# A chunked scan that feeds an FFN: another hand-written list for the lead-in

## The chip, the cores and the metric

The kernel runs on one core of a Trainium2 chip. The metric is the device time of one execution in microseconds; a time of a kernel is the median of its runs. TensorE (PE; its weight loads are shown apart as PEld), VectorE (DVE), ScalarE (ACT), GpSimd (POOL) and SyncE (SP) each work through an instruction list of their own, in order, and wait for one another by semaphores. SyncE here only issues DMAs.

## The reference

The input is a scan with 4 batches of 8 heads over 768 positions, head width 32 and state width 16, and an FFN behind it on 3072 tokens (256 wide, 2048 hidden). Cut to what matters:

```python
log_a = np.log(np.clip(a, 1e-06, 1.0))
for c in range(nc):                       # chunks of positions, in order
    cum = np.cumsum(la, axis=-1)
    L = np.exp(cum[..., :, None] - cum[..., None, :]) * causal
    M = np.einsum('bhin,bhjn->bhij', Cc, Bc) * L
    y[:, :, sl] = M @ xc + (Cc @ state) * np.exp(cum)[..., None]
    state = decay_full * state + sum_j(Bx_j * decay_from_j)
x = y.transpose(0, 2, 1, 3).reshape(B * S, H * D)
h = x @ w_in
return np.maximum(0.01 * h, h) @ w_out
```

## The kernel before

The kernel takes its own chunks of 48 positions, so 16 of them, c = 0 to 15. The steps of a chunk, with the names that the lists use:

- `decN` (L302; `maskN`, L284, and `directN`, L294, for chunks 0 to 2): matmuls that put the sums of log a between two positions into a PSUM bank. `expN` (L321, L326) takes their exponential on ScalarE into `lt`. For chunks from 3 on the operands `dl` and `dr` come back from DRAM (`saveN`, `rowsN`) and are filled on chip (`fl`, `fr`, `cols`).
- `scN` (L347, 16 matmuls of fp32, 32 in the trace): C times B. `weighN` (L361, VectorE) multiplies them into `lt`. `sdN` (L332, GpSimd) puts the state's part into `lt`.
- `pN` (L378, 32 matmuls, 64 in the trace): the products with `xs`, which hold x and, in some rows, the state. `turnN` (L409, VectorE) transposes the new state and `hI` (L422, one of eight copies a chunk, on ScalarE, VectorE or GpSimd) hands it on to the next chunk's `xs`: p2 needs chunk 1's copies.
- `highsN` (L431) and `lowsN` (L439) split a chunk's outputs into a high and a low half, since the FFN is done as three products (high by high, low by high, high by low). The weights of one of the 16 hidden slices arrive packed (`wS`), are decoded by `abs` (L458, ScalarE), `shift` (L471), `sign` (L476) and `low` (L485, VectorE), and are split by `wh` (L496, ScalarE) and `wl` (L499, VectorE or GpSimd).
- `hpS` (L537): slice S of the hidden layer for 512 tokens, six matmuls; `gh`, `act`, `gl` the activation; `opS` (L564) the second product.

Some matmuls do nothing but keep TensorE busy: `du@X:n` is n dummies of 128x512 (`keep_warm`, L139) written into the bank that X will use.

What is done ahead of the main loop is the lead-in. Its order is not planned by a program: `AT_ONCE` (L59) names the DMAs that SyncE issues first, and `LEAD_IN` (L60) is a list of some 300 tokens that a loop (L738 to L753) works through. Each token emits its step, and an engine's list is the order in which the tokens for it were emitted. A letter behind a colon picks the engine (`h6:A`, `wl1:P`). Behind the lead-in (from hp6 on) the main loop sets the order by itself, and the change does not touch it.

PSUM banks are handed out in turn from pools of two: `banks()` (tiles `sc`) and, until the first `hp`, `ps_d` (tiles `pd`). A step that takes a bank waits until the readers of what was last in it are done. `pin`, `pxs` and `wr` hold three chunks of c, three of x and three weight slices.

The fetches on SyncE's queue: `la` 128 KB, each c 448 KB, each w 512 KB, x of chunk 0 256 KB, of later chunks 2 x 96 KB.

The loop that runs the list, for a plain token and for a dummy:

```python
        name, _, host = name.partition("@")
        if host:
            kind = host.rstrip("0123456789")
            keep_warm(space_of(kind, int(host[len(kind):] or 0))[:, 0], int(eng))
            continue
```

Of the kernel before, what the change touches and what calls it, by code (L numbers as in the profile page):

```python
# [55 lines left out]

PD = {0: "d", 1: "d", 2: "d"}
OS = {0: "c", 1: "d", 2: "d"}
AT_ONCE = ["la", "c0", "w0", "x0", "c1"]  # L59
LEAD_IN = """  # L60
less clampn du@mask1:1 lnn clampf reach0:V reach1:V reach3:V top1:P mask0 mask1 after
lnf sums top0:P reach5:V direct0 fl1 sc0 cast0 rest reach2:V revn direct1 reach4:V cast1
exp0 erevn abs0 sd0 du@sc1:2 exp1 part2 fr3:A weigh0 shift0 p0 sel mask2 w1 save0 sc1 x1
fl0 direct2 sign0 c2 turn0 x2 sd1 low0 rows3 h5:P h6:A h3:V h4:P h0:A h2:P h1:A cols
h7:A abs1 weigh1 rev rows4 highs0 shift1 fr4:A sign1 p1 turn1 sd2 sc2 c3 exp2 erevf
du@p2:3 h9:A wh0 lows0 c4 h14:P weigh2 highs1 du@dec3:1 h15:P h13:P dec3 h12:A h8:P dec4
h11:V exp3 h10:V p2 low1 lows1 w2 du@sc3:1 turn2 exp4 highs2 sc3 h22:A rows5 wh1 h21:A
wl0:V h23:A h18:A h20:P lows2 sc4 h17:P x3 abs2 hp0 gh0 sd3 h19:P weigh3 weigh4 wl1:P
hp1 h16:P sd4 act0 shift2 w3 c5 gh1 abs3 dec5 sign2 exp5 gl0 low2 wh2 shift3 act1 sign3
p3 x4 w4 op0 turn3 h29:A low3 h30:P c6 h25:A rows6 highs3 wl2:V sc5 h26:A hp2 h28:A  # L70
h31:P wh3 w5 gl1 op1 h27:A sd5 wl3:P h24:A abs4 gh2 lows3 weigh5 shift4 w6 sign4 act2 p4
save1 turn4 dec6 h35:P h34:P highs4 h33:P h32:P x5 h36:A low4 hp3 abs5 gl2 x6 op2 lows4
wh4 h37:A abs6 w7 rows8 shift5 h38:P wl4:V h39:A c7 gh3 sign5 exp6 shift6 low5 act3 wh5
hp4 gh4 act4 wl5:P rows7 c8 w8 p5 sign6 gl3 turn5 abs7 low6 gl4 sc6 x7 h41:P w9 op3 sd6
highs5 h43:P weigh6 h45:A h42:A h44:P h47:P wh6 wl6:P hp5 h46:P op4 gh5 h40:P act5 lows5
gl5
"""


# [1 line left out]
def scan_ffn(ctx: ExitStack, tc: tile.TileContext, a_l, c_l, x_l, w_l, out_l):  # L81
# [67 lines left out]
    la = pe.tile([128, NC * NM], F32, name="la")  # L149
    for name in AT_ONCE:  # L150
        if name == "la":
# [927 lines left out]
```

## Time and profile before

| | us |
|---|---|
| median of 3 runs (lowest, highest) | 303.19 (302.35, 303.59) |
| profiled execution | 305.16 |
| its span | 302.9 |
| TensorE busy in the span | 296.8 (98%) |
| weight loads of TensorE | 233.0 (77%) |
| VectorE busy | 214.7 (71%) |
| ScalarE busy | 181.8 (60%) |
| GpSimd busy | 66.0 (22%) |

A profile is of one execution. Its span runs from the first instruction to the last; 2.26 us of the execution's own time lie around the span. A busy share is a mean over stages that are limited by different things, so a change in one stage is read from that stage: the timeline of an engine gives, in order, when a group of like instructions starts, how long it takes from its first start to its last end, and in brackets how long the engine idled before it and who ended the wait. Groups overlap a little, because matmuls are pipelined; the distance between two starts is the better price of a group.

### The profile page before, as it was taken

How to read it: one execution, taken by the hardware profiler on the slowest of the kernel's cores; microseconds unless marked ns; L12 is line 12 of the kernel's file. 1: busy time of each engine (PE TensorE's matmuls, PEld its weight loads, DVE VectorE, ACT ScalarE, POOL GpSimd, SP SyncE). 2: the span in 40 equal slices, each digit the busy share in tenths (PEclk: the TensorE clock that was granted, in tenths of full speed). 3: DMA queues.
4: the chain of work that ended last, by engine and by line, in shares of the span. 5: the costliest groups of instructions: out<-in, count | busy, mean ns of one | idle time of the engine just before them, and what ended most of it. 6: DMA issues, size and time to landing. Idle time of an engine off the chain costs nothing.

```text
span 302.9 us, 6809 instructions
## 1 busy us (share of the span) xinstructions
PE 296.8 (98%) x2724; PEld 233.0 (77%) x2724; DVE 214.7 (71%) x379; ACT 181.8 (60%) x348; POOL 66.0 (22%) x141
## 2 busy tenths in 40 slices
PE   8989999999999999999999999999999999999995
PEld 4567777777777778888888888888888888888883
DVE  6589988877676778866877886677566565656562
ACT  4679988576665565835455656673665364536452
POOL 4535565776676430000000000000000000000000
PEclk9999999999999999999999999999999999999999
DMA  7878781965524001000100000000030000000004
GB/s 242 265 214 299 228 263 55 291 193 183 181 89 120 3 2 69 0 2 0 69 2 1 0 0 2 1 0 0 2 139 0 0 2 0 0 1 2 0 0 139
DMA packets 12476, 23.18 MB, mean 77 GB/s; under 512 B 4606, under 2 KB 5502, under 8 KB 12446
## 3 DMA queue, kind: packets, MB, share of 16 engines
q1 hardware_dynamic: 12446, 22.76, 23.5%
q8 instruction: 21, 0.34, 0.4%
q14 instruction: 9, 0.07, 0.1%
HBM read 19.31 MB, written 3.44 MB: 75 GB/s over the span
## 4 chain that ended last, share of the span: by engine, by line
PE 92%; ACT 4%; DVE 2%; issue 1%; DVEq 0%
PE sc L813 18%; PE op L843 14%; PE sc L843 14%; PE op L564 14%; PE hp L537 12%; PE hp L813 7%; PE sc L347 3%; PE sc L378 3%; PE sc L302 1%; ACT xs L422 1%; PE pd L294 1%; PE sc L139 1%; ACT mag L458 1%; PE pd L284 1%; PE pd L378 1%
## 5 line engine op out<-in xcount | busy, mean ns | idle before, releaser
L422 POOL COPY xs<-stage 16x128 f32<-16x128 f32 x96 | 34.5, 360 | 32.4 <-DVE stage L409 24.1
L547 ACT ACTIVATE gh<-hp 128x512 fp32r<-128x512 f32 x32 | 19.1, 597 | 26.8 <-PE hp L537 26.7
L854 ACT ACTIVATE gh<-u 128x512 fp32r<-128x512 f32 x32 | 20.0, 625 | 17.7 <-DVE u L895 17.7
L858 DVE TENSOR_TENSOR gl<-u,gh 128x512 fp32r<-128x512 f32 x32 | 22.0, 687 | 7.9 <-ACT u L855 7.9
L564 PE MATMUL op<-gh,wh 128*128 128x512 f32 x64 | 27.5, 430 | 0.0
L854 ACT ACTIVATE gh<-kept 128x512 fp32r<-128x512 f32 x16 | 10.1, 633 | 28.1 <-DVE kept L903 28.1
L894 DVE TENSOR_TENSOR u<-sc,kept 128x512 f32<-128x512 f32 x16 | 11.1, 691 | 22.2 <-PE sc L813 22.2
L854 ACT ACTIVATE gh<-hp 128x512 fp32r<-128x512 f32 x16 | 9.6, 598 | 26.8 <-PE hp L813 26.8
L564 PE MATMUL op<-gl,wh 128*128 128x512 f32 x64 | 25.1, 392 | 0.0
L564 PE MATMUL op<-gh,wl 128*128 128x512 f32 x64 | 25.0, 391 | 0.0
L843 PE MATMUL op<-gl,wh 128*128 128x512 f32 x64 | 24.9, 389 | 0.0
L843 PE MATMUL sc<-gl,wh 128*128 128x512 f32 x64 | 24.9, 389 | 0.0
L843 PE MATMUL sc<-gh,wl 128*128 128x512 f32 x64 | 24.9, 389 | 0.0
L843 PE MATMUL op<-gh,wh 128*128 128x512 f32 x64 | 24.9, 389 | 0.0
L843 PE MATMUL op<-gh,wl 128*128 128x512 f32 x64 | 24.9, 389 | 0.0
L843 PE MATMUL sc<-gh,wh 128*128 128x512 f32 x64 | 24.9, 389 | 0.0
L903 DVE TENSOR_TENSOR kept<-sc,kept 128x512 f32<-128x512 f32 x16 | 11.1, 692 | 19.4 <-PE sc L813 19.3
L553 DVE TENSOR_TENSOR gl<-hp,gh 128x512 fp32r<-128x512 f32 x32 | 21.7, 677 | 4.3 <-ACT hp L550 4.3
L361 DVE TENSOR_TENSOR lt<-sc,lt 128x384 f32<-128x384 f32 x32 | 16.2, 551 | 12.0 <-ACT gh L547 8.2
L855 ACT ACTIVATE u<-u 128x512 f32<-128x512 f32 x32 | 20.2, 632 | 1.0
L537 PE MATMUL hp<-xh,wh 128*128 128x512 f32 x64 | 20.4, 400 | 0.1
L537 PE MATMUL hp<-xh,wl 128*128 128x512 f32 x64 | 19.9, 392 | 0.0
(142 smaller groups left out, 730.7 us busy)
## 6 DMA issues: line engine op xcount, KB each, us to landing
raw<-w_l SPq DMA_DIRECT2D x16, 512.0 KB
bcn<-c_l SPq DMA_DIRECT2D x16, 448.0 KB
xs<-x_l SPq DMA_DIRECT2D x30, 96.0 KB
out_l<-ob SPq DMA_DIRECT2D x10, 256.0 KB
out_l<-ob SPq DMA_DIRECT2D x4, 128.0 KB
xs<-x_l SPq DMA_DIRECT2D x1, 256.0 KB
dl<-left_d SPq DMA_DIRECT2D x13, 9.0 KB
dr<-right_d SPq DMA_DIRECT2D x13, 9.0 KB
```

Source lines behind the costliest of these rows:

```text
L361: nc.vector.tensor_tensor(out=to, in0=at, in1=to, op=ALU.mult)
L378: nc.tensor.matmul(to[(2 * g + p) * D:(2 * g + p + 1) * D, e, b, cols], lhsT=xs[h * R:(h + 1) * R, 2 * p + e, b], rhs=lt[h * R:(h + 1) * R ...
L422: copy_on(eng)(xss[c + 1][h * R:h * R + N, 2 * p:2 * p + 2, bs], stages[c][rows, :, bs])
L537: nc.tensor.matmul(hp, lhsT=w_half[h][:, f, k * 128:(k + 1) * 128], rhs=x[t][:, k, cols], start=(n == 0), stop=(n == 5),)
L547: nc.scalar.activation(ghs[s], hps[s], AF.Prelu, alpha=0.01)
L553: nc.vector.tensor_tensor(out=gls[s], in0=hps.pop(s), in1=ghs[s], op=ALU.subtract)
L564: nc.tensor.matmul(op, lhsT=w_half[h][:, f, DM + m * 128:DM + (m + 1) * 128], rhs=x, start=(start and i == 0), stop=(last and i == 2),)
L813: nc.tensor.matmul(bank, lhsT=w[h], rhs=x[g], start=start and i == 0, stop=i == 2, skip_group_check=True,)
L843: nc.tensor.matmul(outs[t][m], lhsT=w_half[h][:, f, DM + m * 128:DM + (m + 1) * 128], rhs=x, start=start and i == 0, stop=last and i == 2,)
L854: nc.scalar.activation(gh, h, AF.Prelu, alpha=0.01)
L855: nc.scalar.activation(in_place, h, AF.Prelu, alpha=0.01)
L858: nc.vector.tensor_tensor(out=gl, in0=g, in1=gh, op=ALU.subtract)
```

## The change

Only the two lists differ; every step is done as before, on the same tiles. On SyncE the weight slices w0 and w1 go to the front and chunk 1's c goes behind x0. On GpSimd the zero fill of `top0` comes first, ahead of the selects for `less`; the second fill stays ahead of those for `after`. On ScalarE one fill of `dr` (`fl1`) comes ahead of the logarithms. On TensorE, two dummies come ahead of the first scores, where there were two ahead of chunk 0's products; the mask of chunk 2 comes ahead of chunk 0's products, with a dummy; `revn` comes ahead of `sc0`; chunk 4's decays (`dec4`) come behind chunk 2's products and chunk 3's scores; chunk 4's scores come between `hp0` and `hp1`; chunk 5's decays come behind chunk 3's products. There are seven dummies behind the first four, formerly eight. Of the lead-in's seven `wl`, six now go to GpSimd and wl5 to VectorE; before, wl0, wl2 and wl4 were VectorE's and the others GpSimd's.

```diff
--- before.py
+++ after.py
@@ -56,24 +56,24 @@
 
 PD = {0: "d", 1: "d", 2: "d"}
 OS = {0: "c", 1: "d", 2: "d"}
-AT_ONCE = ["la", "c0", "w0", "x0", "c1"]
+AT_ONCE = ["la", "w0", "c0", "w1", "x0"]
 LEAD_IN = """
-less clampn du@mask1:1 lnn clampf reach0:V reach1:V reach3:V top1:P mask0 mask1 after
-lnf sums top0:P reach5:V direct0 fl1 sc0 cast0 rest reach2:V revn direct1 reach4:V cast1
-exp0 erevn abs0 sd0 du@sc1:2 exp1 part2 fr3:A weigh0 shift0 p0 sel mask2 w1 save0 sc1 x1
-fl0 direct2 sign0 c2 turn0 x2 sd1 low0 rows3 h5:P h6:A h3:V h4:P h0:A h2:P h1:A cols
-h7:A abs1 weigh1 rev rows4 highs0 shift1 fr4:A sign1 p1 turn1 sd2 sc2 c3 exp2 erevf
-du@p2:3 h9:A wh0 lows0 c4 h14:P weigh2 highs1 du@dec3:1 h15:P h13:P dec3 h12:A h8:P dec4
-h11:V exp3 h10:V p2 low1 lows1 w2 du@sc3:1 turn2 exp4 highs2 sc3 h22:A rows5 wh1 h21:A
-wl0:V h23:A h18:A h20:P lows2 sc4 h17:P x3 abs2 hp0 gh0 sd3 h19:P weigh3 weigh4 wl1:P
-hp1 h16:P sd4 act0 shift2 w3 c5 gh1 abs3 dec5 sign2 exp5 gl0 low2 wh2 shift3 act1 sign3
-p3 x4 w4 op0 turn3 h29:A low3 h30:P c6 h25:A rows6 highs3 wl2:V sc5 h26:A hp2 h28:A
-h31:P wh3 w5 gl1 op1 h27:A sd5 wl3:P h24:A abs4 gh2 lows3 weigh5 shift4 w6 sign4 act2 p4
-save1 turn4 dec6 h35:P h34:P highs4 h33:P h32:P x5 h36:A low4 hp3 abs5 gl2 x6 op2 lows4
-wh4 h37:A abs6 w7 rows8 shift5 h38:P wl4:V h39:A c7 gh3 sign5 exp6 shift6 low5 act3 wh5
-hp4 gh4 act4 wl5:P rows7 c8 w8 p5 sign6 gl3 turn5 abs7 low6 gl4 sc6 x7 h41:P w9 op3 sd6
-highs5 h43:P weigh6 h45:A h42:A h44:P h47:P wh6 wl6:P hp5 h46:P op4 gh5 h40:P act5 lows5
-gl5
+top0:P less clampn fl1 mask0 clampf lnn lnf du@mask1:1 fl0 mask1 reach1:V sums cast0
+reach0:V top1:P du@sc0:2 reach4:V reach3:V c1 rest abs0 reach2:V after shift0 cast1
+direct0 part2 revn fr4:A reach5:V exp0 sc0 direct1 sign0 erevn weigh0 du@mask2:1 fr3:A
+mask2 sel low0 exp1 x1 sd0 p0 turn0 sd1 abs1 save0 h1:P h6:P shift1 h5:A h0:P sc1 h4:V
+h3:A weigh1 direct2 h7:A rev c2 h2:A highs0 x2 erevf sign1 p1 turn1 exp2 lows0 sc2 w2
+cols h11:A du@p2:2 h10:A h13:A sd2 h12:P rows3 h15:P h9:P dec3 h8:P weigh2 c3 h14:A wh0
+p2 exp3 low1 rows4 c4 du@dec4:1 turn2 x3 highs1 highs2 rows5 wl0:P lows1 sc3 abs2 dec4
+h19:P lows2 w3 shift2 wh1 exp4 w4 hp0 sign2 save1 h22:A c5 sc4 h23:A rows6 gh0 h16:A
+act0 sd3 wl1:P weigh3 h21:V h17:A h20:P low2 h18:P x4 wh2 weigh4 abs3 gl0 hp1 p3 turn3
+sd4 gh1 wl2:P dec5 w5 abs4 h26:A x5 highs3 shift3 hp2 sign3 op0 h25:P lows3 h24:V h29:A
+act1 h30:A sc5 gh2 exp5 h27:P gl1 low3 shift4 sign4 h31:P w6 act2 wh3 h28:P p4 rows7 c6
+turn4 h32:A op1 gl2 c7 h35:A abs5 low4 sd5 h36:V wl3:P h37:V highs4 wh4 shift5 hp3 wl4:P
+h38:P w7 sign5 h33:A weigh5 c8 low5 gh3 abs6 op2 hp4 h34:P lows4 dec6 act3 h39:A rows8
+shift6 gl3 wh5 gh4 p5 wl5:V exp6 turn5 hp5 highs5 sd6 w8 sign6 h41:P act4 low6 w9 gh5
+h40:P x6 h47:P h44:P gl4 op3 wh6 act5 lows5 h43:P sc6 gl5 x7 op4 h42:P h45:P h46:A wl6:P
+abs7 weigh6
 """
```

The first place is TensorE from the sums (`ends_at`) to chunk 1's scores. `bcn` is a chunk's c, `reach` the decay sums of a chunk, `idle` a dummy's operand. Before (of rows that repeat one stands):

```order
L243 MATMUL sc_101<-ends_at_117,la_106 128x96 x2
L294 MATMUL pd_162<-reach0_125,after_118 64x384 x4
L347 MATMUL sc_180<-bcn_108 64x96 x16
L632 MATMUL sc_101<-la_106,after_118 64x24 x4
L294 MATMUL pd_154<-reach1_126,after_118 64x384 x4
L139 LDWEIGHTS idle_98
L139 MATMUL sc_217<-idle_98 128x512
L378 MATMUL sc_228<-lt_210,xs_112 32x64 x32
L284 LDWEIGHTS bars_120
L284 MATMUL pd_263<-later_119,bars_120 128x384
L347 MATMUL sc_217<-bcn_114 64x96 x16
```

After:

```order
L243 MATMUL sc_101<-ends_at_117,la_106 128x96 x2
L139 LDWEIGHTS idle_98
L139 MATMUL sc_173<-idle_98 128x512
L294 MATMUL pd_156<-reach0_125,after_118 64x384 x4
L632 MATMUL sc_101<-la_106,after_118 64x24 x4
L347 MATMUL sc_173<-bcn_110 64x96 x16
L294 MATMUL pd_162<-reach1_126,after_118 64x384 x4
L139 MATMUL pd_227<-idle_98 128x512
L284 LDWEIGHTS bars_120
L284 MATMUL pd_227<-later_119,bars_120 128x384
L378 MATMUL sc_243<-lt_200,xs_114 32x64 x32
L347 MATMUL sc_288<-bcn_178 64x96 x16
```

Both dummies went from behind `direct1` to ahead of `direct0`; one new dummy and the mask of chunk 2 (`later`, `bars`) now stand ahead of chunk 0's products (`lt`, `xs`).

The second place is TensorE around chunk 2's products. `dl` and `dr` are the operands of the decays, `hp` is a bank of the hidden layer. Before:

```order
L302 LDWEIGHTS dl_123
L302 MATMUL sc_412<-dr_124,dl_123 128x384
L378 MATMUL pd_391<-lt_366,xs_299 32x64 x32
L139 LDWEIGHTS idle_98
L139 MATMUL sc_457<-idle_98 128x512
L347 MATMUL sc_457<-bcn_385 64x96 x16
L347 MATMUL sc_496<-bcn_398 64x96 x16
L537 MATMUL hp_525<-xh_325,wh_144 128x512 x2
L537 MATMUL hp_525<-xl_326,wh_144 128x512 x2
```

After:

```order
L302 LDWEIGHTS dl_123
L302 MATMUL sc_400<-dr_124,dl_123 128x384
L378 MATMUL pd_389<-lt_363,xs_322 32x64 x32
L139 LDWEIGHTS idle_98
L139 MATMUL sc_451<-idle_98 128x512
L347 MATMUL sc_467<-bcn_406 64x96 x16
L302 MATMUL sc_451<-dr_124,dl_123 128x384
L537 MATMUL hp_507<-xh_319,wh_144 128x512 x2
L537 MATMUL hp_507<-xl_320,wh_144 128x512 x2
L537 MATMUL hp_507<-xh_319,wl_145 128x512 x2
L347 MATMUL sc_522<-bcn_449 64x96 x16
```

dec4 (into the bank that now also took the dummy) went behind sc3, and sc4 (the second row of `bcn`) behind hp0; the bank that sc4 gets as sc_522 is the one that sc3 had as sc_467, out of a pool of two.

The third place is VectorE behind chunk 2's products, from the transpose of the new state. `mag` and `top` are the weights in decoding. Before:

```order
L409 STREAM_TRANSPOSE stage_459<-pd_391 128x256
L499 TENSOR_TENSOR wl_145<-w32_303,wh_144 128x512
L439 TENSOR_TENSOR xl_326<-pd_391,xh_325 128x2x128
L439 TENSOR_TENSOR xl_466<-pd_391,xh_465 128x2x64
L361 TENSOR_TENSOR lt_416<-sc_457,lt_416 128x8x48 x2
L361 TENSOR_TENSOR lt_461<-sc_496,lt_461 128x8x48 x2
L471 TENSOR_SCALAR mag_516<-mag_516 128x512
L476 SCALAR_TENSOR_TENSOR top0_146<-raw_455,mag_516 128x512
```

After:

```order
L409 STREAM_TRANSPOSE stage_453<-pd_389 128x256
L439 TENSOR_TENSOR xl_320<-pd_328,xh_319 128x2x192
L439 TENSOR_TENSOR xl_320<-pd_389,xh_319 128x2x128
L439 TENSOR_TENSOR xl_461<-pd_389,xh_460 128x2x64
L471 TENSOR_SCALAR mag_484<-mag_484 128x512
L476 SCALAR_TENSOR_TENSOR top0_146<-raw_384,mag_484 128x512
L361 TENSOR_TENSOR lt_442<-sc_467,lt_442 128x8x48 x2
```

The weighing of chunk 3's scores (`lt_442<-sc_467`), formerly ahead of a slice's decoding, now stands behind the first two steps of it.

## Rows read from the trace of the kernel before

**Rows 1.** The page: busy time (us, share, instructions); instruction queue (packets, MB, share)

```profile
PE 296.8 (98%) x2724; PEld 233.0 (77%) x2724; DVE 214.7 (71%) x379; ACT 181.8 (60%) x348; POOL 66.0 (22%) x141
...
q8 instruction: 21, 0.34, 0.4%
```

**Rows 2.** Stages: us, busy of PE, PEld, DVE, ACT, POOL; clock, DMA, GB/s

```profile
10.05:13.70 3.65, 3.65 (x92) 2.02 (x92) 1.98 (x4) 2.60 (x8) 2.19 (x5) 1.00 0.91 227
...
23.05:43.88 20.83, 20.72 (x326) 15.76 (x327) 19.53 (x36) 19.48 (x46) 11.23 (x21) 1.00 0.83 260
43.88:299.00 255.12, 255.12 (x1985) 205.49 (x1983) 178.88 (x299) 147.38 (x266) 44.25 (x92) 1.00 0.14 45
```

**Rows 3.** TensorE's timeline up to sc1: start us, us, line, operation, count

```profile
6.87 1.55 PE L347 MATMUL sc<-bcn 32*64 32x96 f32 x32
...
8.59 1.54 PE L294 MATMUL pd<-reach,after 48*64 48x384 f32 x8
10.06 1.03 PE L139 MATMUL sc<-idle 128*128 128x512 bf16 x2
11.03 1.18 PE L378 MATMUL sc<-lt,xs 64*32 64x64 f32 x64
12.14 0.82 PE L284 MATMUL pd<-later,bars 112*128 112x384 bf16 x2
12.89 1.26 PE L347 MATMUL sc<-bcn 32*64 32x96 f32 x32
```

**Rows 4.** TensorE's timeline from p1 to behind hp1

```profile
15.53 0.86 PE L378 MATMUL pd<-lt,xs 64*32 64x64 f32 x64
16.32 0.89 PE L347 MATMUL sc<-bcn 32*64 32x96 f32 x32
17.14 0.82 PE L139 MATMUL pd<-idle 128*128 128x512 bf16 x3
17.80 0.38 PE L139 MATMUL sc<-idle 128*128 128x512 bf16 x1
18.01 0.94 PE L302 MATMUL sc<-dr,dl 102*128 102x384 bf16 x4
18.88 0.90 PE L378 MATMUL pd<-lt,xs 64*32 64x64 f32 x61
20.83 0.30 PE L378 MATMUL pd<-lt,xs 64*32 64x64 f32 x3 [1.05 <-issue]
21.06 0.39 PE L139 MATMUL sc<-idle 128*128 128x512 bf16 x1
21.38 1.55 PE L347 MATMUL sc<-bcn 32*64 32x96 f32 x64
23.06 0.70 PE L537 MATMUL hp<-xh,wh 128*128 128x512 f32 x2
...
25.93 0.50 PE L302 MATMUL sc<-dr,dl 102*128 102x384 bf16 x2
```

**Rows 5.** Queue of instructions, 13.0 to 14.5 and 18.0 to 19.5: packets, MB, share

```profile
q8 instruction: 1, 0.02, 4.5%
...
q8 instruction: 1, 0.02, 3.9%
```

**Rows 6.** Timelines of ScalarE and VectorE, steps behind p2 in the weights' and scores' chain

```profile
21.72 0.54 ACT L431 CAST xh<-pd 128x256 fp32r<-128x256 f32 x2 [1.49 <-DVE stage L409]
...
24.18 0.68 ACT L458 ACTIVATE mag<-raw 128x512 bf16<-128x512 bf16 x1
...
17.34 1.02 DVE L361 TENSOR_TENSOR lt<-sc,lt 128x384 f32<-128x384 f32 x2
...
25.37 1.31 DVE L476 SCALAR_TENSOR_TENSOR top<-raw,mag 128x512 uint16<-128x512 uint16 x1
...
27.76 0.28 DVE L471 TENSOR_SCALAR mag<-mag 128x512 uint16<-128x512 uint16 x1
28.08 0.75 DVE L476 SCALAR_TENSOR_TENSOR top<-raw,mag 128x512 uint16<-128x512 uint16 x1
```

## The prediction

> **What bounds the kernel now.** First the shares of busy time: TensorE is busy 98% of the span [rows 1]. The stages then say where the other 2% lie [rows 2]: from 43.88 us, where hp6 begins, to 299.00 TensorE is busy 255.12 of 255.12 us, and in the 20.83 us before that it idles 0.11. So whatever moves the start of hp6 moves the end by as much; the change is worth what it does to that one number, now 43.88. Going back along TensorE's timeline there is one hole: chunk 2's products, p2, stop after 61 of their 64 pairs (weight load and matmul) and go on at 20.83, after 1.05 us in which no semaphore was waited for ("issue") [rows 4].
>
> **What that hole is** decides the case. The instruction queue brings 21 packets, 0.34 MB [rows 1], so 16 KB each, and TensorE alone has 2724 matmuls and as many weight loads: about 259 instructions a packet. I take a block for 128 pairs. Counted back from the stop through 61 of p2, 4 of decays, 4 dummies and 32 of sc2 [rows 4], the block before began 27 pairs ahead of p1's end, about the 37th pair, at 15.53 + 0.42 = 15.95; the one before that, by the same count (p1's 37, rev's 4, direct2's 8, sc1's 32, mask2's 2), at about p0's 19th pair, near 11.3. One packet was fetched between 13.0 and 14.5 and one between 18.0 and 19.5 [rows 5]: each some 2 us after TensorE entered a block, bringing the next. So a block seems usable 20.83 − 15.95 = 4.9 us after the one before it was entered; the earlier was usable in 15.95 − 11.3 = 4.65 at most, since p1 shows no stop.
>
> The Trainium skill says otherwise: "Runtime: NRT & Kernel Launch", section "Instruction fetch mechanics", has 256 instructions in a 16 KiB block, as counted here, and calls the cost of crossing "mostly hidden". The 1.05 us [rows 4] speak against the second half; as a rival it is priced below.
>
> **The change, part by part.**
>
> *TensorE before p1.* Up to the sums the lists are alike (5 dummies, 4 mask matmuls, 4 sums). Then after has two dummies before sc0, one before mask2 and none directly before p0: one more. Two took 11.03 − 10.06 = 0.97 [rows 3], so +0.49. mask2 (0.75, 12.14 to 12.89) now comes before p0. So p0 starts at 11.03 + 0.49 + 0.75 = 12.25, 1.2 later; p1 only about 0.3 later, 15.8, since what is pushed past 13.7 runs at the higher clock: sc0's 32 matmuls took 1.49 us, sc2's 0.82, though the granted clock in [rows 2] is 1.00 from 10.05 to 13.70 as behind 23.05; here durations show the two levels, 1.2 and 2.4 GHz, and that column does not. revn ahead of sc0 costs nothing in sum.
>
> *p1 and p2.* p0's 16th pair (12.25 + 0.2) now opens the block: the next one is usable at 12.45 + 4.65 = 17.1 at the latest, and p1 wants it at its 36th pair, 15.8 + 0.4 = 16.2. That is a new stop of 0 to 0.9; I take 0.6, nearer the upper end, because 4.65 and 4.9 agree so well. Then 16.8 + 4.9 = 21.7 for the next block. Where does that one begin? Before: 6 dummies behind the sums, 4 decay matmuls (dec3, dec4) and 61 of p2 lie ahead of the stop, 71 in all; after: 5 + 2 + 64 = 71, and all else is the same. So p2 is now just complete and the dummy behind it is stopped. p2 itself: p1 ends at 15.8 + 0.8 + 0.6 = 17.2, and 18.88 − 16.32 = 2.55 later p2 could begin as before, ending at 20.6 (19.75 if the two fewer dummies and dec4 shorten that stretch), before 21.7 either way. So removing dummies and dec4 there gains nothing: the block covers it. The dummy runs at 21.7 instead of 21.06: **+0.65**.
>
> *Behind the stop.* dec4 (18.01 to 18.88 for two such, 0.43 each [rows 4]) now stands here: **+0.43**. sc4 moves from behind sc3 to behind hp0: nothing by itself, but its bank is now the one of chunk 3's scores, so it waits until DVE has done weigh3, and DVE has lows1, lows2, shift2 and sign2 queued before that; hp1, p3 and all of TensorE stand behind sc4. From p2's end P, in [rows 6]: highs2 ends at P + 1.13 (21.13 to 22.26), then abs2 0.68, shift2 0.28, sign2 0.75, weigh3 1.02: P + 3.86, at 24.5 for P = 20.6. hp0 ends at 21.7 + 0.32 (dummy) + 0.82 (sc3) + 0.43 (dec4) + 1.43 (half of 23.06 to 25.93) = 24.7. No wait, by 0.2 to 1.0 us. dec3's exponentials, for whose bank sc3 now waits, are over by about 20.
>
> *Transfers, GpSimd, fills.* w0 and w1 now go ahead of x0: 1856 KB up to x0's last byte, at the 260 GB/s of [rows 2] 7.3 us, so about 8.5; p0 wants it at 12.25, and sc1 wants c1 (2304 KB, about 10) at 13.3. A zero fill ahead of the selects delays them by well under 1 us, and direct0, their first user, itself starts one us later. More low halves (wl) go to GpSimd, which is busy 11.23 of 20.83 us [rows 2]; its slack hides them, and without it each would hold an hp by at most its own length. I count all at 0, and for the rest up to hp6 the time of before.
>
> Sum: +0.65 + 0.43 = +1.1. The profiled execution took 305.16 us (span 302.9), so it would come to 306.3; it stands 1.97 above the median of three, 303.19, and the same shift of that gives **304.3 us** (its own range 303.8 to 305.0, for a stop in p1 of 0.1 to 0.9 and up to 0.4 of small waits).
>
> **Rivals.**
> *The block for p1 comes in time* (no stop there: its delay may be anything under 4.65): 15.8 + 0.4 + 4.9 = 21.1, so +0.05 + 0.43: 303.7. For it: p1 showed no stop before. Against: the slack was under 0.3 us if the delay is like the next one's. Chance 0.20.
> *Blocks are hidden throughout*, and the 1.05 us were an accident: p2 ends at 19.1 to 20.0, the dummy runs 1.1 to 2 us sooner; dec4 gives back 0.43, and sc4 then waits for weigh3: P + 3.86 against P + 3.0, 0.86. Sum −0.7 to +0.2: 302.9. This is where the Trainium skill's sentence leads. Chance 0.12.
> *The two early dummies bring the higher clock sooner*, say from direct1 on instead of 13.7: by the differences of the same shapes that saves up to 1.9 us before p1. If blocks stop TensorE it only waits for them longer (p0 enters its block at 11.6; +4.65 + 4.9 gives 21.1, 303.7, inside the first rival). If they don't, it adds about −1.6 to the case before: 301.3. Chance of that 0.10.
> *Slower: sc4's wait comes on top.* The point is P = 20.9: if p2 ends later (a few pairs of it behind the stop, as before, or a longer stop in p1), weigh3 is the later one. With p2's last pairs behind the stop, P = 21.95: weigh3 ends at 25.8, hp0 at 24.95, so 0.2 + 0.9 more: 305.4. For it: the count of 71 is exact to one or two instructions only, and sign2 took 1.31 at its slowest instead of 0.75 [rows 6]. Chance 0.16.
> The forecast keeps 0.42.
>
> **How the numbers follow.** 8 in 10 leaves out the fast case (0.10) and the far end of the slow one: 301.9 to 305.8. About 0.5%, 1.5 us, is what a measurement of this kernel tells from no change: faster is below 301.7, slower above 304.7. Slower: 0.16 and a third of the forecast's 0.42, 0.30. Faster: 0.10 and a quarter of the hidden case, 0.13. Same: 0.57.
>
> **What would show it.** In the changed kernel's profile: p0 near 12.25 and p1 near 15.8; a hole by "issue" in the middle of p1, 0.6 us; p2 whole, then a hole by "issue" up to about 21.7 ahead of the dummy; no idle time, or little, before sc4; hp6 near 45.0. Wrong would be: the halving of durations well before 13.7, no "issue" holes, or sc4 idle on DVE's weighing.

## The result and the profile after

The changed kernel is slower: 306.4 us, the median of 6 runs (304.38 to 307.69), against 302.77 of before (301.74 to 303.59), a ratio of 1.0107 (95% interval 1.0077 to 1.0137). Measured again with the experiments it took 306.03 against 302.86, 1.0085 (1.0048 to 1.0122). The forecast was 304.3 with a range up to 305.8: the direction of its sum was right and its size a third of what was measured; "slower" had been given 0.30. Medians here are of all executions; ratios and the spans further down leave out those over 1.5% above the quickest of their kernel (9 of 138 of before).

The profiled execution of the changed kernel is the quickest of its six, 304.38 us with a span of 302.0, and it is shorter than the profiled one of before (305.16, span 302.9). The two profiles taken side by side would thus say "faster by 0.8 us". Why that is misleading is the first thing to be found out. The page's line of busy time, beside [rows 1]:

```profile
PE 293.9 (97%) x2723; PEld 232.0 (77%) x2723; DVE 212.9 (70%) x379; ACT 181.1 (60%) x347; POOL 69.1 (23%) x142
```

By stages (columns as in [rows 2]: length, busy time of PE, PEld, DVE, ACT and POOL, granted clock, DMA share, GB/s):

```profile
9.40:13.35 3.95, 3.12 (x109) 2.16 (x109) 2.57 (x7) 2.27 (x7) 2.15 (x6) 1.00 1.02 290
...
17.38:18.72 1.34, 0.01 (x2) 0.01 (x1) 1.12 (x3) 1.34 (x5) 1.20 (x2) 1.00 0.69 188
18.72:43.04 24.32, 23.54 (x394) 17.77 (x394) 20.33 (x42) 20.32 (x46) 15.84 (x25) 1.00 0.83 260
43.04:298.00 254.96, 254.96 (x1985) 205.55 (x1983) 178.29 (x298) 147.04 (x265) 42.26 (x89) 1.00 0.14 44
```

From hp6 on (43.04) TensorE is busy without a break, as in [rows 2], and the same 259.0 us pass from there to the end of the span as before (302.9 − 43.88 = 259.0, 302.0 − 43.04 = 259.0). So everything is decided ahead of hp6, as the prediction had it. But the stage from the end of the hole behind p2 to hp6 takes 24.32 us with 0.78 idle; before, from the dummy behind p2 to hp6 (21.06 in [rows 4] to 43.88), it took 22.82. TensorE's timeline up to the end of p4 (start, length, line, count, idle time before and its releaser), beside [rows 3, 4]:

```profile
9.41 0.85 PE L378 MATMUL sc<-lt,xs 64*32 64x64 f32 x64 [0.17 <-DMA xs<-x_l]
11.08 0.89 PE L347 MATMUL sc<-bcn 32*64 32x96 f32 x32 [0.82 <-DMA bcn<-c_l]
...
13.35 1.08 PE L378 MATMUL pd<-lt,xs 64*32 64x64 f32 x64
...
16.45 0.93 PE L378 MATMUL pd<-lt,xs 64*32 64x64 f32 x64
18.72 0.39 PE L139 MATMUL sc<-idle 128*128 128x512 bf16 x1 [1.33 <-issue]
19.04 0.89 PE L347 MATMUL sc<-bcn 32*64 32x96 f32 x32
19.86 0.50 PE L302 MATMUL sc<-dr,dl 102*128 102x384 bf16 x2
...
21.67 0.89 PE L347 MATMUL sc<-bcn 32*64 32x96 f32 x32
...
24.07 0.71 PE L378 MATMUL sc<-lt,xs 64*32 64x64 f32 x47
24.98 0.35 PE L378 MATMUL sc<-lt,xs 64*32 64x64 f32 x17 [0.19 <-issue]
25.26 0.50 PE L302 MATMUL sc<-dr,dl 102*128 102x384 bf16 x2
...
28.43 0.89 PE L347 MATMUL sc<-bcn 32*64 32x96 f32 x32
29.26 0.91 PE L378 MATMUL sc<-lt,xs 64*32 64x64 f32 x62
30.75 0.30 PE L378 MATMUL sc<-lt,xs 64*32 64x64 f32 x2 [0.58 <-issue]
```

In the kernel before, p3 and p4 run through:

```profile
26.36 0.86 PE L378 MATMUL sc<-lt,xs 64*32 64x64 f32 x64
...
32.51 0.86 PE L378 MATMUL sc<-lt,xs 64*32 64x64 f32 x64
```

Three things are to be seen. p0 runs at 9.41 for 0.85 us where [rows 3] had 11.03 and 1.18: the matmuls' durations halved at about 5.7 us in this execution, not at 13.7. p2 is whole and the stop stands right behind it, ahead of the dummy, as the count of 71 said. And there are two more stops "by issue", inside p3 and p4, where before had none. They stand at the starts of instruction blocks: from the dummy at 18.72 to the stop at 24.98 lie 1 + 32 + 2 + 6 + 32 + 6 + 47 = 126 pairs, from there to the one at 30.75 17 + 2 + 6 + 6 + 32 + 62 = 125 (sc4 and the groups of six hp or op matmuls counted in; a few semaphore instructions fill up the 256). The instruction queue says the same: it began to fetch a packet at 16.15, 22.61 and 28.46 us, and TensorE went on 2.57, 2.37 and 2.29 us later; in the profile of before it was 18.42 and 2.41. In all profiles below, a stop at the start of a block ended 2.2 to 2.9 us after the start of such a packet.

Counted that way in both traces, TensorE entered its blocks at 11.26, 15.92, 20.83, 26.79, 33.05 and 40.26 before and at 9.54, 13.99, 18.72, 24.98, 30.75 and 41.20 after. From the third entry to the sixth it took 19.4 us before and 22.5 after; these are not the same operations, so the difference is not the loss, which the table below gives. The changed list has put short instructions (products, scores: 64 or 32 pairs in 0.8 us) into the two blocks behind p2, whose work is done before the next one is there, and the long ones (hp, op: six pairs in 1.4 us) into the block behind them, which takes 10.4 us.

By groups, from start to start, for the same operations between the dummy behind p2 and hp6:

| us | before | after |
|---|---|---|
| scores (4 chunks) | 3.32 | 3.29 |
| decays (before 2, after 3 chunks) | 0.64 | 0.83 |
| hp | 8.69 | 8.92 |
| products p3, p4, p5 | 2.54 | 3.70 |
| op | 7.31 | 7.26 |
| dummy | 0.32 | 0.32 |
| sum | 22.82 | 24.32 |

Of the 1.50 us, 1.16 lie in the products: p3 and p4 take 1.33 more, p5 0.17 less.

### The profile page after: what moved, and what is told of

The parts are those of the page before. It is cut to its first block, busy times and chain, and to the rows that moved or that the text cites. A ratio compares the mean times of both kernels' runs of the same rounds, so it can differ in the third digit from the quotient of the medians.

```text
span 302.0 us, 6817 instructions
## 1 busy us (share of the span) xinstructions
PE 293.9 (97%) x2723; PEld 232.0 (77%) x2723; DVE 212.9 (70%) x379; ACT 181.1 (60%) x347; POOL 69.1 (23%) x142
## 3 DMA queue, kind: packets, MB, share of 16 engines
HBM read 19.31 MB, written 3.44 MB: 75 GB/s over the span
## 4 chain that ended last, share of the span: by engine, by line
PE 94%; DMA 3%; issue 1%; SPq 1%; DVE 0%; POOL 0%; ACT 0%; POOLq 0%
PE sc L813 18%; PE op L564 15%; PE hp L537 15%; PE op L843 14%; PE sc L843 14%; PE hp L813 7%; PE sc L378 4%; PE sc L347 3%; DMA bcn<-c_l 3%; PE sc L302 2%; PE pd L378 1%; POOL xs L422 0%; SPq L113 0%; PE pd L294 0%; PE pd L639 0%
## 5 line engine op out<-in xcount | busy, mean ns | idle before, releaser
L903 DVE TENSOR_TENSOR kept<-sc,kept 128x512 f32<-128x512 f32 x16 | 11.1, 692 | 19.5 <-PE sc L813 19.3
L499 POOL TENSOR_TENSOR wl<-w,wh 128x512 fp32r<-128x512 f32 x15 | 20.4, 1368 | 7.5 <-ACT wh L496 6.7
```

The source lines that it names most:

```text
L499: eng.tensor_tensor(out=wl[:, f], in0=w32s[f], in1=wh[:, f], op=ALU.subtract)
```

## The experiments

Eighteen runs (sixteen edits, and the two kernels once more), each with its own executions and with those of before on the same chip. The mean granted clock of every execution is listed with its span. That number begins with the first record of the clock, so the low start of the profile of before doesn't show in it (1.00 in [rows 2]); where it is below 0.997, the clock is taken to have fallen again later, as in the profiles with such a number. Medians of spans in us:

| kernel | time, median (before, same job) | clock 0.997 or more: number, span | below: number, span |
|---|---|---|---|
| before, all jobs | 302.5 to 303.4 | 98, 300.5 | 31, 301.5 |
| changed, e1 and first | 306.0, 306.4 | 5, 302.8 | 10, 304.2 |
| e3 | 306.22 (302.86) | 4, 303.2 | 6, 304.6 |
| e4 | 306.56 (302.86) | 5, 303.2 | 7, 304.7 |
| e5 | 303.14 (303.27) | 8, 300.8 | 3, 302.0 |
| e6 | 303.21 (303.27) | 10, 301.2 | 0 |
| e7 | 307.41 (303.27) | 1, 303.4 | 5, 305.9 |
| e8 | 303.16 (303.27) | 4, 300.2 | 7, 301.7 |
| e9 | 305.68 (303.40) | 9, 303.6 | 1, 303.8 |
| e10 | 304.19 (303.40) | 8, 301.7 | 4, 303.0 |
| e11 | 306.03 (303.40) | 6, 303.3 | 6, 304.2 |
| e12 | 302.52 (303.40) | 10, 300.2 | 1, 301.4 |
| e13 | 307.04 (302.48) | 2, 302.5 | 4, 305.2 |
| e14 | 303.83 (302.48) | 11, 301.7 | 1, 303.6 |
| e15 | 304.33 (302.48) | 6, 302.3 | 6, 302.4 |
| e17 | 307.54 (302.56) | 0 | 6, 305.6 |
| e18 | 307.90 (302.56) | 0 | 6, 306.0 |

### The two kernels again (e1, e2)

No edit.

> The changed kernel itself, for a second profile and the mean granted clock of every execution. Theory 1 (the clock comes early but does not stay): most executions have a mean granted clock of 0.992 to 0.994 and take 306 to 307 us, and their profile has a stretch of some 5 us, in the first 30, in which the durations of matmuls are doubled; the rare ones with 1.000 take about 304.4. Theory 2 (the stops for instruction blocks are longer in the usual execution than in the profiled one): clock 1.000 also at 306, with holes by issue that sum to over 4 us, where the first profile has 2.1.

> The kernel before, unchanged, for a second profile. Its first profiled execution took 305.16 us while six others had a median of 302.77. Theory 1: the usual execution of before has its clock up earlier than 13.7 us (mean granted clock 1.000 all the same, since it counts from the first record), so that hp6 begins about 2 us before 43.88, and the time is 302 to 303.5. Theory 2: the clock again comes at 13.7 and the 2.4 us lie in the holes by issue or outside the span.

e1: 306.03 us; its profile has a mean clock of 0.994. The view of cores, the clock by stretches, and TensorE's timeline from p1:

```profile
core 0: 303.4 us, clock 0.994
```

```profile
21.10:24.50 3.40, 3.40 (x16) 2.33 (x18) 1.95 (x4) 1.70 (x5) 2.30 (x4) 0.50 0.83 278
```

```profile
12.68 0.64 PE L378 MATMUL pd<-lt,xs 64*32 64x64 f32 x38
14.53 0.44 PE L378 MATMUL pd<-lt,xs 64*32 64x64 f32 x26 [1.21 <-issue]
...
16.98 0.95 PE L378 MATMUL pd<-lt,xs 64*32 64x64 f32 x64 [0.33 <-POOL xs L422]
19.81 0.39 PE L139 MATMUL sc<-idle 128*128 128x512 bf16 x1 [1.89 <-issue]
...
21.21 1.31 PE L537 MATMUL hp<-xh,wh 128*128 128x512 f32 x2
```

The stop in p1 that the forecast had as 0 to 0.9 is there with 1.21, and 126 pairs behind it (26 + 32 + 2 + 2 + 64) the one behind p2, with 1.89; then, from 21.1 to 24.5, the granted clock is 0.50 (hp0's first two matmuls take 1.31 us instead of 0.77). In this execution no block stops p3 or p4: from the dummy to hp6 it takes 24.62 us without idle time, 10.28 of them in hp (8.92 in the first profile). Theory 1 holds as far as it goes: by their mean clock 10 of 15 executions of the changed kernel have such a stretch, 31 of 129 of before. But the 5 without it are also 2.3 us longer than those of before, so the clock is not the main part. Theory 2 is half right: the stops by issue differ from execution to execution.

e2 took 303.51 us with a profile of 305.38, in which durations halve at 13.45. So the profiled execution of before was again one with a late clock. The stop in p2 was 1.85 instead of 1.05:

```profile
18.76 0.90 PE L378 MATMUL pd<-lt,xs 64*32 64x64 f32 x61
21.51 0.30 PE L378 MATMUL pd<-lt,xs 64*32 64x64 f32 x3 [1.85 <-issue]
```

### The early part: fetches, dummies, mask (e3, e4, e5, e11, e12)

e3 is the changed kernel with the first fetches of before:

```diff
-AT_ONCE = ["la", "w0", "c0", "w1", "x0"]
+AT_ONCE = ["la", "c0", "w0", "x0", "c1"]
-... reach4:V reach3:V c1 rest ...
+... reach4:V reach3:V w1 rest ...
```

> The changed kernel with the fetch order of before (c0, w0, x0, c1, w1). Its TensorE waits 0.17 us for x0 and 0.82 us for c1 in the first profile, with p0 at 9.41 and sc1 at 11.08. Theory 1: without the two waits the clock has less reason to fall, so at least half of the executions have 1.000, and the median is 303 to 305. Rival (the low clock comes of something else, the dummies behind or the later stop of 1.33 us): the same 306 and the same 0.992, since the 0.99 us are given back at the stop for the next instruction block.

306.22 us: no gain. Its profile waits neither for x0 nor for c1, and then stops for 1.22 in p1 and for 1.61 behind p2. The rival holds: what the two waits cost is given back at the next block.

e4 moves the changed kernel's early dummies, e5 those of the kernel before the other way:

```diff
e4: -... top1:P du@sc0:2 reach4:V ... du@mask2:1 fr3:A ...
    +... top1:P reach4:V ... du@mask2:3 fr3:A ...
e5: -... reach5:V direct0 ... sd0 du@sc1:2 exp1 ...
    +... reach5:V du@sc0:2 direct0 ... sd0 exp1 ...
```

> The changed kernel with the two early dummies moved from ahead of the first scores to ahead of the mask of chunk 2, so three there. Theory 1: the clock comes later, as in the kernel before, once and for good; mean granted clock 1.000, median 302.5 to 304. Rival (the loss is in dec4, sc4 and the stops, not in the dummies): 306 as the changed kernel.

> The kernel before with one edit: its two dummies ahead of chunk 0's products go ahead of the first scores, as in the changed kernel. Theory A (the early dummies bring the clock up early, and it is lost again in some executions): profile with the clock up near 6 us, p0 near 9, a stop in p1 of about 1.2 us and one behind it, median 303 to 306, mean granted clock often 0.994. Theory B (the dummies' place is of no weight; the loss is in the order behind p2): median 302 to 303.5, as before.

e4 306.56, e5 303.14 (ratio to before 0.9986, 0.9952 to 1.0020): by the times, the dummies' place is of no weight, and theory A's 303 to 306 falls. The one profiled execution of e5, of 305.65 us, does look as theory A said, with the clock up at 7.1, two stops and a mean clock of 0.994, though it has the order of before behind p2:

```profile
14.59 0.43 PE L378 MATMUL pd<-lt,xs 64*32 64x64 f32 x25 [0.68 <-issue]
...
20.60 0.30 PE L378 MATMUL pd<-lt,xs 64*32 64x64 f32 x3 [2.17 <-issue]
```

Nor are the dummies needed for an early clock: without them ahead of the first scores durations halve at 13.5 to 14.0 us in the profiles of before, e2, e4 and e14, but at 4.2 to 6.4 in seven others (5.9, 4.8 and 6.1 in e6, e8 and e12). With them they halve at 4.0 to 7.1 in all nine profiles, so that the dummies make an early clock likelier is neither shown nor excluded. e4 is of use for another reason: its profile has the late clock (14.0) and can be laid beside that of before. It has the stop behind p2 and the one in p4:

```profile
21.24 0.39 PE L139 MATMUL sc<-idle 128*128 128x512 bf16 x1 [1.36 <-issue]
...
33.16 0.30 PE L378 MATMUL sc<-lt,xs 64*32 64x64 f32 x2 [0.63 <-issue]
```

The dummy runs at 21.24 (21.06 in [rows 4]), hp6 at 45.45 instead of 43.88: 24.2 us lie between, and the loss of that profile, 1.5 us, is nearly all behind p2.

e11 undoes the mask's move in the changed kernel, e12 makes it in the kernel before:

```diff
e11: -... weigh0 du@mask2:1 fr3:A mask2 ... sd0 p0 turn0 ...
     +... weigh0 fr3:A ... sd0 p0 du@mask2:1 mask2 turn0 ...
e12: -... shift0 p0 sel mask2 w1 ...
     +... shift0 du@mask2:1 mask2 p0 sel w1 ...
```

> The changed kernel with one part undone: chunk 2's mask and its dummy go behind chunk 0's products again. Theory D: chunk 0's products enter their instruction block 0.5 to 1 us sooner and all blocks behind follow, so the median falls by about as much, to 305 to 305.6, and the stop behind p2 ends near 18 us where the clock is up early. Theory C: no gain, 306, because the blocks that stop TensorE behind p2 are unchanged.

> The mirror: the kernel before, with chunk 2's mask and one more dummy ahead of chunk 0's products. Theory D: 0.5 to 1 us slower than before, 303.6 to 304.2, with the stop in p2 ending later by as much. Theory C: within 0.4 us of before.

e11 306.03: no gain. e12 302.52 (0.9985, 0.9953 to 1.0016): no loss. Theory D falls. e12's profile shows the early part of before at the higher clock:

```profile
9.33 0.86 PE L378 MATMUL sc<-lt,xs 64*32 64x64 f32 x64
...
13.16 0.82 PE L378 MATMUL pd<-lt,xs 64*32 64x64 f32 x60 [0.20 <-DMA xs<-x_l]
...
14.51 0.89 PE L347 MATMUL sc<-bcn 32*64 32x96 f32 x32 [0.52 <-DMA bcn<-c_l]
...
17.06 0.93 PE L378 MATMUL pd<-lt,xs 64*32 64x64 f32 x64
17.93 0.39 PE L139 MATMUL sc<-idle 128*128 128x512 bf16 x1
```

p0 is as early as in the changed kernel, p1 waits for x1 and sc2 for c2, but no block stops p1 or p2, and the dummy runs at 17.93, 0.8 sooner than in the changed kernel's quickest execution. From there to hp6 (41.16) it took 23.2.

### Chunk 4's decays and the dummies behind chunk 2's scores (e6, e7, e8)

e6 moves `dec4 exp4` behind `sc3` in the kernel before; e7 undoes that in the changed kernel and takes sc4 back ahead of hp0; e8 takes four dummies out of the kernel before.

```diff
e6: -... h8:P dec4 h11:V exp3 ... turn2 exp4 highs2 sc3 h22:A ...
    +... h8:P h11:V exp3 ... turn2 highs2 sc3 dec4 exp4 h22:A ...
e7: -... dec3 h8:P weigh2 ... sc3 abs2 dec4 ... shift2 wh1 exp4 w4 ... c5 sc4 h23:A ...
    +... rows4 ... dec3 h8:P dec4 weigh2 ... p2 exp3 exp4 ... sc3 abs2 ... lows2 sc4 ...
e8: -du@p2:3 h9:A ... du@dec3:1 h15:P ...
    +h9:A ... h15:P ...
```

> The kernel before with one edit: chunk 4's decays and their exponentials go behind chunk 2's products and chunk 3's scores, as in the changed kernel; sc4 stays ahead of hp0 and so waits for what frees its bank. Theory B: the stop inside p2 stays where it is in time (about 4.9 us after p1 entered its block), dec4 then adds its 0.43 behind it, and sc4 may wait: median 303.3 to 304.5. Theory A: within 0.3 us of before, 302.9.

> The changed kernel with one part undone: chunk 4's decays ahead of chunk 2's products and chunk 4's scores ahead of hp0 again. Theory B: the block stop hides dec4 again, so 0.43 and what else is lost behind p2 comes back: median 305 to 305.6, or 303 to 304 if most of the 3.2 us is lost there. Theory A: 306 as the changed kernel, with the low clock in most executions.

> The kernel before without the four dummies between chunk 2's scores and its decays (0.87 us of TensorE's time; nothing is computed by them). If the instruction block sets the resumption: p2 is complete before the stop, which falls four pairs later, right behind it; the resumption is still about 4.9 to 5.3 us after p1 entered its block, so the time gains at most 0.23 us: 302.5 to 303. If not: p2 ends 0.87 sooner, median 302.0.

e6 303.21 (0.9998, 0.9972 to 1.0025): dec4's place doesn't move the median. Its profile has 1.26 us by issue ahead of sc4, 35 pairs behind the start of a block and so no stop of this kind. sc4 there follows dec4 into a pool of two banks, so it takes the bank of chunk 3's scores, and it starts 0.11 us after VectorE has weighed these (19.31 + 1.01 = 20.32):

```profile
19.31 1.01 DVE L361 TENSOR_TENSOR lt<-sc,lt 128x384 f32<-128x384 f32 x2
20.43 0.89 PE L347 MATMUL sc<-bcn 32*64 32x96 f32 x32 [1.26 <-issue]
```

By the bank and the times that is the wait for weigh3 of the prediction's last rival, in another kernel than the changed one. The equal medians don't say that it is free: e6's ten spans lie between 300.8 and 301.6, those of before in the same job, at 0.997 or more, between 299.8 and 303.3.

e7 307.41: taking dec4's move back in the changed kernel doesn't help either; its products for chunk 2 stop after 62 pairs, for 2.13 us, 126 pairs behind the stop in p1. So both theories A and B fall here; the loss must lie in what else the list orders. e8 303.16 against 303.27: 0.87 us less of TensorE's work and no gain, as an instruction block that sets the time would have it. Its profile, however, has no stop by issue but waits of 1.07 for x1, 0.90 for c2 and 0.65 for VectorE, and the clock at 0.50 from 15.0 to 21.8, so it shows only that this time is covered twice.

### The two halves of the list (e9, e10)

e9 is the order of before up to p2, then the changed order for all tokens that are left; e10 the reverse, with dec4 right behind p2.

```diff
e9:  up to p2 as before, then
+ w2 low1 du@dec4:1 turn2 x3 highs2 rows5 wl0:P lows1 sc3 abs2 h19:P lows2 w3 shift2 wh1 exp4 ...
e10: up to p2 as changed, then
+ rows4 c4 highs1 dec4 exp3 low1 lows1 du@sc3:1 turn2 exp4 highs2 sc3 h22:A rows5 wh1 h21:A ...
```

> A list put together from both: up to chunk 2's products as before, behind them the changed list's order of what is left. Theory C (the loss lies behind p2: there the changed order packs products and scores closer, so that later instruction blocks stop TensorE again, 24.3 us from p2's resumption to hp6 instead of 22.8): about 1.0 to 1.5 us slower than before, median 304 to 304.7, stops by issue inside p3 or p4. Theory D (the loss lies ahead of p2: chunk 0's products come later, so every block does): as before, 302.9 to 303.3.

> The other half: the changed list up to chunk 2's products, behind them the order of before of what is left (with dec4 right behind p2). Theory C: 0.5 to 1 us slower than before for the dec4 and the later block, 303.5 to 304.2. Theory D: 305 to 306. The time that lies outside the span, 2.3 us in the changed kernel and its variants and 1.86 in the kernel before and its variants, goes with one of the two halves.

In e9 the dummy that belongs ahead of dec4 falls behind it and overwrites chunk 4's decays; the work is the same. e9 took 305.68 us (1.0086, 1.0052 to 1.0119), e10 304.19 (1.0029, 0.9998 to 1.0060). So the order behind p2 (with the engines of its copies and low halves) is the larger part: taking it back gains some 2 us of the 3.2 (e11, measured beside e10 and close to the changed kernel, took 306.03), and putting it in costs 2.3, though e9 has waits of its own at the seam (0.71 and 0.79 for VectorE, 0.91 and 0.46 for ScalarE) and no stop by issue, so that its sum is not that of the changed kernel. Theory C holds for the place, not yet for the reason. e10 keeps both things that the forecast had priced, the later block for p2 and dec4 behind it, and loses 0.8 us, not clear of its interval (1.3 by the spans at 0.997 or more, 301.7 against 300.4 in the same job). Its profile still has the stop in p1, and p3 and p4 without stops; from the dummy ahead of sc3 to hp6 it took 22.97 us, about as before (22.82):

```profile
14.67 0.44 PE L378 MATMUL pd<-lt,xs 64*32 64x64 f32 x26 [1.22 <-issue]
...
18.97 0.48 PE L302 MATMUL sc<-dr,dl 102*128 102x384 bf16 x2 [0.91 <-PE pd L378]
```

### Chunk 4's products alone (e13, e14)

e13 takes p4 in the changed kernel behind op1, e14 takes it ahead of op1 in the kernel before.

```diff
e13: -... p4 rows7 c6 turn4 h32:A op1 gl2 ...
     +... rows7 c6 op1 p4 turn4 h32:A gl2 ...
e14: -... gl1 op1 h27:A sd5 wl3:P h24:A ... lows3 ... p4 save1 turn4 ...
     +... gl1 h27:A h24:A lows3 p4 turn4 op1 sd5 wl3:P ... save1 ...
```

> The changed kernel with one step moved: chunk 4's products (and what follows from them, their transpose and one copy) go behind op1, as in the kernel before, instead of ahead of it. Theory E (behind p2 the changed order packs 128-pair blocks of short matmuls so closely that the next block isn't there): the stop of 0.58 us in p4 goes, median 0.4 to 0.6 below the changed kernel, 305.4 to 305.8; in executions whose clock fell behind p2 there is no such stop and nothing to gain. Rival F (the loss is small waits for other engines in that order): no change, 306 to 306.3, the stop moves to the next group.

> The mirror: the kernel before with chunk 4's products ahead of op1 (two copies of the state and chunk 3's low halves moved ahead of them so that they can run). Theory E: p4 comes 1.4 us sooner and nearer to sc5, and stops by issue for 0.3 to 0.8 in executions with an early clock; median 0.2 to 0.6 above before. Rival F: within 0.3 us of before.

e13 took 307.04 against 302.48. The stop in p4 is gone, and the last pair of an hp waits for GpSimd's half of the weights instead:

```profile
31.30 0.86 PE L378 MATMUL sc<-lt,xs 64*32 64x64 f32 x64
...
36.64 0.73 PE L537 MATMUL hp<-xh,wl 128*128 128x512 f32 x2 [0.42 <-POOL wl L499]
```

From the dummy behind p2 to hp6 it is 24.2 us still (19.58 to 43.76). Both theories are right in part: the block stops p4 as E says, and behind it, as F says, the changed order has another wait ready. e14 took 303.83 (1.0047, 1.0009 to 1.0085): 1.3 us lost by moving p4 forward by one op, but its profile shows a wait for a copy on ScalarE, not for a block:

```profile
32.69 0.85 PE L378 MATMUL sc<-lt,xs 64*32 64x64 f32 x64 [1.08 <-ACT xs L422]
```

### Attempts on the data queue, and at a faster kernel (e15 to e18)

e15 and e18 start from e12. e15 fetches x1 and c2 ahead of w1, e16 puts the whole DMA order of before into the changed kernel, e17 (from before) and e18 fetch c4 and w2 behind rows5.

```diff
e15: -... sel w1 save0 sc1 x1 ... sign0 c2 ...
     +... sel x1 c2 w1 save0 sc1 ... sign0 ...
e16: -AT_ONCE = ["la", "w0", "c0", "w1", "x0"]; then c1 x1 save0 c2 x2 w2 rows3 c3 rows4 c4 x3 rows5 ...
     +AT_ONCE = ["la", "c0", "w0", "x0", "c1"]; then w1 save0 x1 c2 x2 rows3 rows4 c3 c4 w2 rows5 x3 ...
e17: -... lows0 c4 h14:P ... lows1 w2 du@sc3:1 ... rows5 wh1 ...
     +... lows0 h14:P ... lows1 du@sc3:1 ... rows5 c4 w2 wh1 ...
```

> An attempt at a faster version: the kernel before with chunk 2's mask and a dummy ahead of chunk 0's products (the run of 302.5) and with x1 and c2 fetched ahead of w1. The profiles of before's kind with an early clock waited 0.5 to 1.0 us for x1 and c2. If these waits set p2: 0.4 to 0.7 below before, 302.2 or less where before is near 303. If the next block sets it: no change.

> The changed kernel with the whole DMA order of before on SyncE's queue (x1 behind the sums' way out, w2 behind the rows and c4, and so on), all other engines' lists as changed. Theory G (TensorE's instruction blocks are fetched by the same DMA engines, so a fuller data queue between 8 and 17 us brings them later): the fetches for p1 and p2 start 1.1 to 1.3 us after TensorE entered a block instead of 2 to 2.8, the stop in p1 goes, median 305 to 305.4. Theory H (the DMA order is of no weight for them): 306 to 306.4 with the same stops.

> An attempt at a faster version: the kernel before with c4 and w2 fetched behind rows5, so that 960 KB less are under way between 12 and 18 us, when the block that p2 needs is fetched. Theory G: the stop in p2 shrinks by 0.5 to 1 us, median 0.4 to 0.9 below before. Theory H: as before; if c4 or w2 come late, 0.5 slower.

> The same with chunk 2's mask and one dummy ahead of chunk 0's products as in the run with 302.5. Theory G: 0.4 to 1.2 below before. Theory H: within 0.5 of before.

e15 took 304.33 (1.0045, 1.0016 to 1.0074): the waits for x1 and c2 are gone, and two stops by issue stand in their place, 126 pairs apart:

```profile
14.13 0.43 PE L378 MATMUL pd<-lt,xs 64*32 64x64 f32 x26 [0.68 <-issue]
...
19.30 0.30 PE L378 MATMUL pd<-lt,xs 64*32 64x64 f32 x4 [1.34 <-issue]
```

This is the clearest case of waits that hid others: with them gone the kernel is 1.85 us slower than before. Why the stops are longer than e12's waits (0.20 and 0.52) isn't shown. e16 took 311.66: its profile has stops of 1.26 and 1.61 as the changed kernel, and the fetches began 2.6 and 2.5 us after TensorE had entered a block, not 1.1 to 1.3, so theory G (the data queue's fill) has no support there; in this list rows8 land in the slot of chunk 6's decay rows before those are used, so dec6 computes with chunk 8's rows, and it waits 1.22 us for them. e17 (307.54) and e18 (307.9) don't test G either, since c4 came too late:

```profile
PE sc L347 <- DMA bcn<-c_l: 3.6, 2, 2.9
```

(The waits of TensorE in e17: releaser, us, times, longest.) None of the tries beats the kernel before by more than its interval; e12, the best, is at 0.9985 (0.9953 to 1.0016).

## Why the prediction was wrong

**What bounds the kernel** was right: hp6's start carries through to the end, 258.9 to 259.0 us in all twenty profiles. **The hole** was read rightly too: in all profiles the long idle times by issue inside or behind p1, p2, p3 and p4 stand some 126 pairs apart, where a block begins (or twice that, as in e4), and end 2.2 to 2.9 us after a packet of the instruction queue started; e6's wait ahead of sc4 is another thing. That is the best supported part. What the Trainium skill says ("Runtime: NRT & Kernel Launch", section "Instruction fetch mechanics": mostly hidden) holds for the rest of these programs but not for the first 35 us, with up to three stops of 0.2 to 2.2 us.

**Ahead of p2.** The place of the stop behind p2 came as said. p0 came at 9.41, not 12.25, since the clock was early; where it was late (e4) p0 came at 12.57, 1.54 later than before, 0.47 of it a wait for c0. The stop in p1 (0 to 0.9, taken as 0.6) is missing in the changed kernel's profile (p1 only stretched to 1.08) and was 1.21 in e1 and 1.22 in e3. That this costs time was not borne out by single edits: mask and dummies are worth nothing (e5, e11, e12). The list up to p2, with dec4 behind it, costs 0.8 us in the median (e10), not clear of its interval; the forecast had +0.65 and +0.43 for the two.

**Behind p2: the step that failed.** "I count all at 0, and for the rest up to hp6 the time of before" left out 1.1 us at full clock: 24.32 instead of 22.82 + 0.43 (24.21 in e4). dec4 itself took 0.20 there, not 0.43. The prediction had the period of the blocks, 4.9 us or more for 128 pairs, and the order of the operations behind p2, but applied the one to the other only as far as p2. Counting on to the next two blocks would have put their starts into p3 and p4. There the trace stops for 0.19 and 0.58 (0.63 in e4), and where a stop is avoided (e13) GpSimd's low halves, counted at nothing, hold hp for 0.42. e10 is the run that shows the place: with the order of before behind p2, 2 of the 3.2 us are back. That the blocks are the reason is read from the full-clock profiles; no run took away these stops alone and got the time back (e13 took one away), and in e1, with the low clock in their place, they don't occur.

**The baseline.** "The same shift" from the profiled execution to the median took for granted that the profile shows the usual execution. It doesn't: its clock came at 13.7 us, and all prices ahead of p2 were read from that; in e6, e8 and e12, of the same early order, it came at 4.8 to 6.1. The sign was in the table: 305.16 stood 1.6 above the highest of the three runs, and nothing asked why. Of before's 98 spans at 0.997 or more, 73 lie between 299.5 and 301.7 (median 300.2) and 25 between 302.2 and 303.6; both profiles of before (302.9, 303.5) are of the second kind. Beside a profile of equally late clock (e4, hp6 at 45.45 against 43.88) a sum of +1.1 would have been near, at +1.5, but by luck: the dummy ran 0.2 later there, not 0.65, and 1.4 was lost behind it, not 0.43.

**The clock's falls** were in no case of the prediction. 10 of 15 executions of the changed kernel have one, and these are 1.4 us longer than its others; of before 31 of 129, 1.0 longer. That makes 0.67 × 1.4 − 0.24 × 1.0 = 0.7 us of the difference of the medians. With 2.3 at full clock (302.8 − 300.5), and 0.45 by which time less span is larger (2.32 against 1.87, medians of the same job), it is 3.4, near the 3.2 and 3.6 measured. This is an estimate from medians, not a separation by experiment.

**The rivals.** sc4's wait for weigh3 did not occur in the changed kernel: no idle time stands before sc4 at 21.67, as the forecast had it; in e6 it did, for 1.26. "The early dummies bring the clock" gives no time (e4, e5), and seven profiles have an early clock without them; in the profiles of e4 and e5 themselves it went as that rival says (14.0 and 7.1). "The block comes in time" happened in the profiled execution, where p1 shows no stop.

**What stays open.** Why a block comes 4 to 4.5 us after the one before in e6 and e12 and 4.7 to 6 in the changed kernel and its kin; e15 and e16 speak against the data queue's order as the sole reason. It lies in when a fetch starts: 1.2 to 1.6 us after the block ahead was entered for the first three of e6, 2.0, 2.2, 3.9 and 3.5 us for the first four of the changed kernel; what sets that isn't shown. Why the clock falls more often in the changed kernel: in e1, e3, e5 and e11 it fell within 1.3 us of the end of a stop by issue, but not after 2.13 us in e7. And why its time outside the span is larger; e10, with the order of before behind p2, is at 1.83 and e9 at 2.04, but in that job before itself was at 2.18.

## What to carry to other kernels

Count instructions, not only their time: where many short instructions follow one another, the next block of the program can be what the engine waits for, and it shows as idle time by "issue" at a fixed count of instructions. Count all the way along the list, not only as far as the place that the change was made for, and expect that a wait removed ahead of such a place buys nothing (e3, e8, e15). Whether spreading short groups among long ones helps isn't shown: e13 did it for one group, and the kernel got no faster. Before pricing anything from a profile, check that its own time lies among the other runs; if it doesn't, find out in which way it is unusual.

## What the runs showed of the hardware

The clock's rise differs between executions of one order: durations halved at 13.5 to 13.7 us in three profiles that begin as before (before, e2, e14), at 4.2 to 6.4 in seven others with the same beginning. It can fall back to 0.50 from 21.1 to 24.5 us with TensorE busy all through that stretch (3.40 of 3.40 in e1), 1.3 us after a stop of 1.89 us had ended. The mean granted clock shows only the second of these. And an instruction block's arrival varies between executions of one kernel: the stop in p2 was 1.05 and 1.85 us in two profiles of before, and the changed kernel stopped in p1 for 1.21 us in e1 and not at all in its first profile.
